# Fewer table passes on VectorE and ScalarE: sums by accumulating DMA, mixing on TensorE, contiguous kernel rows and a new instruction order in a gated mix of two long convolutions

## The chip, the cores and the metric

One core of a Trainium2 chip. The metric is device time in microseconds (us) of one execution; three runs of the kernel before took 291.55, 291.79 and 292.98, median 291.79. The engines are named as in the profile: PE is the matrix engine (PEld its weight loads), DVE the vector engine, ACT the scalar engine, POOL and SP the two others, which here build constants and issue DMAs.

## The reference

The input `x = A_u` (2048 steps, 448 channels) goes through two long convolutions, and a gate mixes them:

```python
x = A_u
g = sigmoid((x * gate_w).sum(-1, keepdims=True))
# A: kernel K[d, l] = Re sum_n C[d,n] * exp(dt*A[d,n] * l) * dt*B[d,n],  n = 0..255
a = causal_conv(x, K) + x * Dskip
# B: kv = (4-tap causal shift of k) * v
b = x * (causal_conv(kv, ssm_k) + kv * ssm_D)
out = g * a + (1 - g) * b          # bf16
```

The reference does the convolutions by real FFTs of length 4096.

## The kernel before, in words

Channels are cut into four quarters H = 0 to 3 of 112, that is NC = 28 columns on each of four groups; M = 8 x 28 = 224. The 2048 steps lie as 32 x 64. A convolution is a hand-made FFT by matmuls: `spread` (line 339) and `transform` (351) go forward, `swapped` (670) swaps real and imaginary halves by SP's DMAs, `products` (392) multiplies on DVE, `stage_a` (368) and `stage_b` (379) come back. Every result in PSUM (`ps`, four rooms of two banks) is taken out by an `evac`, a copy that class `Copies` (322) puts on ACT, or on DVE where the string `COPIES` has a V.

For convolution A the kernel rows must first be made, in one table per quarter (`table`, 842). `KGen.exps` (410) and `KGen.reals` (417) are exponentials on ACT of a (128, 224) row each: `reals` makes NR = 16 rows R[i] = exp(8(2i+1) x). `levels` (421) makes sines on ACT from phases on DVE. `tables` (471) builds two tables of 32 complex rows in bf16, TQ and TP, on DVE: `product` (439) multiplies n rows by one complex entry and leaves the four real products, `add` (446) sums them in pairs. Rows 8 to 15 of TP are such sums of four rows each, twice 128 x 1792 elements. `back` (464) makes rows 16 to 31 from rows 15 to 0, times R. `sums` (510) contracts TQ with TP on PE, `gather` (527) interpolates the result into kernel rows KT, laid out (b, r, n), and `cols` (566) gives `spread` row n of it, 64 elements that lie 28 apart, as weights. R and KT share the tile RK.

`mix` (876) does the mixing for a quarter: the window of `ug` (tile natv; it holds b) is multiplied by `og` = 1 - g, the window of `uu` (tile natu; it holds a) by `gb` = g, and they are added. For the last quarter `epilogue_A` (818) multiplies by g straight from PSUM, adds, and stores.

`Consts` (174) builds the transform matrices at the start: POOL writes integer ramps, DVE turns them into phases (`phases`, 203; used by `stage_2`, 224, and `stage_b`, 250, in passes of 128 x 1024), ACT takes sines. Where ACT goes from exponentials to sines or back, the trace has an ACT_TABLE_LOAD.

The order of the work is written out by hand. Every engine call is recorded (`Order`, 123), and the string `ORDER` gives the sequence in which they are issued; `issue` (130) chains the calls of one engine, SP's and POOL's among them, so each engine runs them in this order. `SLOTS` and `ROOMS` say which of six SBUF buffers (`q`) and four PSUM rooms each use gets. `PLAN` says in which order the parts are recorded: tables T, convolutions B and A, and mixing m. As all calls are issued at one place, the profile gives every instruction the same line, 135; the tile tells them apart.

Of the kernel before, what the change touches and what calls it, by code (L numbers as in the profile page):

```python
# [37 lines left out]
    "02143540432152033255104414002511354023"  # L38
)
ROOMS = (  # L40
    "102312011321221213030023033232221120301102302321010101233332311322223113013221223223032100113132320001003030031120131221"
    "11120010230212303030103220332020232303031012110011322201031010322120303131222023"
)
COPIES = (
    "SSVSSSSSSSSSSSSSSSSSSSSSSSSSSSSSSSSSSSSSSSSSSSSSSSSSSSSSSSSSSSSSSSSSSSSSSSSSSSSSSSSSSSSSSSSSSSSSSSSSSSSSSSSSSSSSSSSVVSSS"
    "SSSSSSSSSSSSSSSSSSSSSSSSSSSSSSSSSSSSSSSSSSSSSSSSSSSSSSSSSSSSSVSSSSVSSS"
)
ORDER = (
# [53 lines left out]
)  # L102

# [70 lines left out]
class Consts:  # L174
# [49 lines left out]
    def stage_2(self, b_col, off_col, room):  # L224
# [3 lines left out]
        for k0 in (0, 16):  # L228
            if k0:
                for r in range(2):  # L230
                    nc.vector.scalar_tensor_tensor(out=off_col[r], in0=b_col, scalar=32.0 * k0, in1=off_col[r], op0=ALU.mult, op1=ALU.add)
# [699 lines left out]
```

## Time and profile before

| what | value |
|---|---|
| median of three runs | 291.79 us |
| the profiled execution | 293.36 us, of it span 291.0 us |
| mean granted TensorE clock | 0.875 |
| DMA | 20.92 MB in 56755 packets, mean 72 GB/s |
| POOL | 53 instructions, 9.9 us, all in the first 37 us |
| DVE's longest waits | 7.0 us for PE, 5.5 for ACT (four), 4.7 for a DMA, all on tile q |
| stores | from about 277 us on; nothing but DMA after 280.4 us |

The page has the busy time and share of each engine; the span in 40 slices; the DMA queues; the chain that ended last, followed back from the end, with its share by engine; the costliest groups of instructions, as "line engine operation out<-in shapes xcount | busy us, mean ns of one | idle time before them and what ended it"; and DMA issues, with KB and us to landing. The trace behind it gives the same by stretch of time, by tile, or in order of time.

### The profile page before, as it was taken

The page shows a single profiled execution, that of the slowest core. Times are in us where ns is not written, and L with a number is a line of the kernel's source. Part 1 is how long each engine was busy: PE and PEld are TensorE (multiplying, and loading weights), DVE is VectorE, ACT ScalarE, POOL GpSimd, SP SyncE. Part 2 cuts the span into 40 slices and gives each one's busy share as a digit, 9 for nine tenths or more (in the row PEclk, how much of TensorE's full clock was granted, in tenths as well). Part 3 has the DMA queues.
Part 4 walks back from the last instruction along what each step waited for, and adds up shares of the span by engine and source line. Part 5 has one row for each costly group of instructions (what it writes and reads, how often), then busy time and mean ns, then how long its engine had stood idle before and what let it go on. Part 6 is the DMA issues. An engine that isn't in the chain of part 4 may idle for free.

```text
span 291.0 us, 12305 instructions
## 1 busy us (share of the span) xinstructions
PE 219.8 (76%) x5599; PEld 203.9 (70%) x5599; DVE 242.2 (83%) x374; ACT 224.3 (77%) x322; POOL 9.9 (3%) x53
## 2 busy tenths in 40 slices
PE   0155786878796998997699988687998967899820
PEld 0144775777786988996698978587998956789720
DVE  8869999999997699999789997893999985524950
ACT  3378949799887889999779899993999994268600
POOL 9100200000000000000000000000000000000000
PEclk9995879778796997999979999998999799669955
DMA  6999924915761002522300000622000036100067
GB/s 174 178 198 190 144 94 74 176 39 106 119 146 36 5 2 34 124 71 66 83 5 2 5 2 2 149 61 52 2 5 3 2 81 144 37 5 2 2 134 121
DMA packets 56755, 20.92 MB, mean 72 GB/s; under 512 B 49280, under 2 KB 56192, under 8 KB 56704
## 3 DMA queue, kind: packets, MB, share of 16 engines
q1 hardware_dynamic: 52192, 18.65, 34.5%
q10 hardware_dynamic: 4512, 1.49, 2.4%
q8 instruction: 44, 0.72, 1.0%
q14 instruction: 7, 0.06, 0.1%
HBM read 8.17 MB, written 2.52 MB: 37 GB/s over the span
## 4 chain that ended last, share of the span: by engine, by line
PE 35%; ACT 27%; DVE 22%; issue 7%; DMA 5%; POOL 0%; SPq 0%; ACTq 0%; DVEq 0%; POOLq 0%
PE ps L135 35%; ACT q L135 20%; DVE TP L135 6%; DVE TQ L135 4%; ACT RK L135 4%; DVE natv L135 3%; DMA q<-in_A_C_im_dram 2%; DVE q L135 2%; DMA q<-in_A_B_re_dram 2%; ACT ET L135 2%; DVE PH L135 1%; DVE ET L135 1%; DVE G L135 1%; ACT natu L135 1%; DVE RK L135 1%
## 5 line engine op out<-in xcount | busy, mean ns | idle before, releaser
L135 ACT CAST q<-ps 128x1024 bf16<-128x1024 f32 (+4 forms) x160 | 135.2, 937 | 8.5 <-PE ps L135 8.1
L135 PEld LDWEIGHTS <-q 128*128 128x128 bf16 (+2 forms) x720 | 56.0, 149 | 18.1 <-DMA q<-in_A_B_re_dram 13.5
L135 DVE TENSOR_TENSOR TQ<-TQ,ET 128x896 bf16<-128x896 bf16 (+1 forms) x56 | 44.6, 818 | 0.0
L135 PE MATMUL ps<-q,s_W 128*128 128x112 bf16 (+1 forms) x544 | 36.2, 221 | 10.9 <-ACT q L135 10.8
L135 PEld LDWEIGHTS <-s_W 128*128 128x128 bf16 x544 | 30.8, 103 | 15.3 <-issue 12.9
L135 PE MATMUL ps<-TP,TQ 128*32 128x32 bf16 x1792 | 32.8, 242 | 11.2 <-issue 9.9
L135 DVE TENSOR_TENSOR q<-q,q 128x3584 bf16<-128x3584 bf16 (+1 forms) x22 | 32.4, 1509 | 10.3 <-DMA q<-q 4.7
L135 PEld LDWEIGHTS <-TQ 128*32 128x32 bf16 x1792 | 30.7, 155 | 13.3 <-issue 12.3
L135 PEld LDWEIGHTS <-natu 128*32 128x32 bf16 (+1 forms) x560 | 30.4, 182 | 11.8 <-DMA natu<-in_B_k_dram 6.0
L135 PE MATMUL ps<-sa_R,q 128*128 128x128 bf16 x448 | 37.8, 250 | 1.0 <-ACT q L135 0.7
L135 DVE TENSOR_TENSOR TP<-TP,ET 128x3584 bf16<-128x3584 bf16 (+2 forms) x20 | 30.7, 1552 | 0.0
L135 PE MATMUL ps<-q,G 128*128 128x28 bf16 x1024 | 27.9, 176 | 2.3 <-ACT q L135 2.3
L135 PEld LDWEIGHTS <-G 128*128 128x128 bf16 x1024 | 27.2, 97 | 3.3 <-issue 2.6
L135 ACT ACTIVATE RK<-hold 128x224 bf16<-128x224 f32 x64 | 22.9, 410 | 3.5 <-DVE hold L135 1.4
L135 PE MATMUL ps<-q,natu 128*32 128x224 bf16 (+3 forms) x336 | 18.9, 332 | 8.7 <-DMA natu<-in_B_k_dram 5.4
L135 ACT CAST RK<-ps 128x896 bf16<-128x896 f32 (+1 forms) x15 | 10.9, 749 | 18.2 <-PE ps L135 18.2
L135 ACT ACT_TABLE_LOAD x16 | 20.5, 1283 | 2.0 <-PEq L915 1.7
L135 PE MATMUL ps<-Wc,natv 128*64 128x128 bf16 x224 | 16.1, 293 | 4.0 <-DVE natv L135 2.6
L135 PEld LDWEIGHTS <-natv 128*64 128x64 bf16 x224 | 15.6, 212 | 4.4 <-DVE natv L135 2.7
L135 PE MATMUL ps<-q,q 128*32 128x336 bf16 (+3 forms) x112 | 17.7, 329 | 1.2 <-DMA q<-in_B_k_dram 1.2
L135 ACT ACTIVATE ET<-PH 128x1344 bf16<-128x1344 int16 (+1 forms) x12 | 17.6, 1465 | 1.2 <-DVE PH L135 1.1
L135 DVE TENSOR_TENSOR TP<-TP 128x1792 bf16<-128x1792 bf16 (+4 forms) x22 | 18.0, 830 | 0.0
(76 smaller groups left out, 272.1 us busy)
## 6 DMA issues: line engine op xcount, KB each, us to landing
q<-q SPq DMA_DIRECT2D x64, 112.0 KB, 2.4
sk<-in_B_ssm_k_dram SPq DMA_DIRECT2D x16, 112.0 KB, 3.5
natv<-in_B_v_dram SPq DMA_DIRECT2D x4, 448.0 KB, 8.0
natu<-in_A_u_dram SPq DMA_DIRECT2D x4, 448.0 KB, 5.7
out_dram<-natv SPq DMA_DIRECT2D x8, 112.0 KB, 4.4
out_dram<-natv ACTq DMA_DIRECT2D x8, 112.0 KB, 4.8
xfd<-q SPq DMA_DIRECT2D x1, 672.0 KB, 3.3
hold<-xfd SPq DMA_DIRECT2D x2, 336.0 KB, 2.9
```

The source lines that it names most:

```text
L135: ins = f(*args, **kw)
```

## The change

Six edits, in one program.

1. Rows 8 to 11 and 12 to 15 of TP are no longer summed by DVE. `split` lets the product write one half of the real products into the rows themselves and the other half into rows 16 and up, and a DMA of POOL's queue adds the second to the first (`accum_op`). `back(8, 16)`, which needs rows 0 to 7, now stands ahead of `back(0, 8)`, which needs rows 8 to 15. There are two such DMAs in each of four tables.
2. `reals` takes 8 exponentials and one factor exp(128 x) on ACT, and DVE makes the other 8 rows by one product.
3. `og` is gone. A matrix `minus` = -identity is made once, and `stage_b` of convolution A begins each bank with a matmul of `minus` and the window of `ug`, so that PSUM holds a - b; `mix` multiplies by g and adds b. For the last quarter the passes with `og` go too.
4. KT is laid out (n, b, r), so that a kernel row is 64 elements in a row.
5. `Copies` becomes `Sides`: it also puts the phases of `stage_2` and `stage_b` on DVE or ACT. The string has 198 letters for what was 190 (eight phases more); four of the eight phases are on ACT, and six copies on DVE instead of five.
6. `SLOTS`, `ROOMS`, the string of sides and `ORDER` are all new, so that every engine's sequence changes, the loads on SP and the table loads on ACT (21 instead of 16) among them.

```diff
+    def line(self, dst, src, mult, add):
+        if self.vector():
+            self.nc.vector.tensor_scalar(out=dst, in0=src, scalar1=mult, scalar2=add, op0=ALU.mult, op1=ALU.add)
+        else:
+            self.nc.scalar.activation(dst, src, ACT.Identity, scale=mult, bias=add)
...
-def stage_b(nc, places, G, U, consume, banks=2):
+def stage_b(nc, places, G, U, consume, banks=2, less=None):
...
+            if less is not None:
+                for i in range(0, n, 16):
+                    nc.tensor.matmul(pt[:, h + i // 16, 0:448].rearrange("p (b c) -> p b c", c=NC), lhsT=less[0], rhs=less[1](b0 + 16 * h + i, 16),
+                                     start=True, stop=False)
...
     def reals(self, H):
-        for i in range(NR):
+        for i in range(NR // 2):
             self.nc.scalar.activation(self.R[:, i], self.hold[:, H % 2, 0], ACT.Exp, scale=float(8 * (2 * i + 1)))
+        self.nc.scalar.activation(self.R[:, NR], self.hold[:, H % 2, 0], ACT.Exp, scale=128.0)
+        self.nc.vector.tensor_tensor(out=self.R[:, 8:16], in0=self.R[:, 0:8], in1=self.R[:, NR].unsqueeze(1).to_broadcast([P, 8, M]), op=ALU.mult)
...
+    def split(self, dst, base, src, n, e):
+        T, r = self.TP, self.ET[:, ENTRY[e], 1]
+        o, s = T[:, dst], T[:, src]
+        part = list(o.ap[0])
+        self.nc.vector.tensor_tensor(
+            out=bass.AP(o.tensor, o.offset, [part, [2 * M, n], [M, 2], [(base - dst) * 2 * M, 2], [1, M]]),
+            in0=bass.AP(s.tensor, s.offset, [part, [2 * M, n], [0, 2], [M, 2], [1, M]]),
+            in1=bass.AP(r.tensor, r.offset, [list(r.ap[0]), [0, n], [-M, 2], [M, 2], [1, M]]), op=ALU.mult)
+        flat = lambda a: T[:, a:a + n].rearrange("p n c m -> p (n c m)")
+        self.nc.gpsimd.dma_start(out=flat(dst), in_=flat(base), accum_op=ALU.add)
...
-        p(16, 0, 4, 64)
+        self.split(8, 16, 0, 4, 64)
         add(TQ, 3, 15, 2, -2)
-        add(TP, 8, 16, 4)
         q(27, 1, 2, -1, 512)
-        p(24, 4, 4, 64)
+        self.split(12, 20, 4, 4, 64)
         add(TQ, 7, 27, 2, -2)
-        add(TP, 12, 24, 4)
         q(27, 5, 2, 2, 512)
+        self.back(8, 16)
+        add(TQ, 8, 27, 2)
         self.back(0, 8)
-        add(TQ, 8, 27, 2)
-        self.back(8, 16)
...
-                self.evac(KT[:, :, r + 1 - per:r + 1, w0:w1], room.rearrange("p r (b n) -> p b r n", b=8))
+                self.evac(KT[:, w0:w1, :, r + 1 - per:r + 1], room.rearrange("p r (b n) -> p n b r", b=8))
...
-        return self.KT[:, :, :, c].rearrange("p b r -> p (b r)")
+        return self.KT[:, c].rearrange("p b r -> p (b r)")
...
+    minus = wp.tile([P, P], bf16, name="minus")
+    V.tensor_scalar(out=minus[:], in0=ident, scalar1=-1.0, scalar2=None, op0=ALU.mult)
...
+    less = lambda H: (minus[:], lambda b0, n: window(ug, b0, n, H))
...
         if H == NQG - 1:
             V.tensor_tensor(out=o, in0=o, in1=x, op=ALU.mult)
-        weighed(o, og)
-        if H < NQG - 1:
-            weighed(x, gb)
-            V.tensor_tensor(out=o, in0=o, in1=x, op=ALU.add)
+            return
+        V.tensor_tensor(out=paired(x), in0=paired(x), in1=gb[:].unsqueeze(2).to_broadcast([P, 64, NC // 2, 2]), op=ALU.mult)
+        V.tensor_tensor(out=o, in0=o, in1=x, op=ALU.add)
```

More of the change, by code (lines that the diff above doesn't have):

```diff
@@ L37 @@
 SLOTS = (
-    "02143540432152033255104414002511354023"
+    "20134425014243155430102242331052105431"
 )
 ROOMS = (
-    "102312011321221213030023033232221120301102302321010101233332311322223113013221223223032100113132320001003030031120131221"
-    "11120010230212303030103220332020232303031012110011322201031010322120303131222023"
-)
-COPIES = (
-    "SSVSSSSSSSSSSSSSSSSSSSSSSSSSSSSSSSSSSSSSSSSSSSSSSSSSSSSSSSSSSSSSSSSSSSSSSSSSSSSSSSSSSSSSSSSSSSSSSSSSSSSSSSSSSSSSSSSVVSSS"
-    "SSSSSSSSSSSSSSSSSSSSSSSSSSSSSSSSSSSSSSSSSSSSSSSSSSSSSSSSSSSSSVSSSSVSSS"
+    "201203313031210032010020112210211213301123120030012333111101212122223332022113030333011103101230332230110323321100113330"
+    "00111301233103100130202120333303303332010030223122101210213321310131103103032103"
+)
+SIDES = (
+    "VSSSVVSVSSSSSSSSSSSSSSSSSSSSSSSSSSSSSSSSSSSSSSSSSSSSSSSSSSSSSSSSSSSSSSSSSSSSSSSSSSSSSSSSSSSSSSSSSVSSSSSSSSSSSSSSSSSSVSSS"
+    "VSSVSSSSSSSSSSSSSSSSSSSSSSSSSSSSSSSSSSSSSSSSSSSSSSSSSSSSSSSSSSSSSSSVSVSSSSSSSS"
 )
 ORDER = (
[53 rows of a table removed]
[51 rows of a table added]
 )
@@ L174, with __init__ @@
 class Consts:
-    def __init__(self, nc, pool, scratch):
-        self.nc, self.pool = nc, pool
+    def __init__(self, nc, pool, scratch, sides):
+        self.nc, self.pool, self.sides = nc, pool, sides
         self.scratch, self.used = scratch, 0
@@ L228, in stage_2 @@
         for k0 in (0, 16):
+            off = off_col
             if k0:
+                off = [self.carve(1).bitcast(f32) for _ in range(2)]
                 for r in range(2):
-                    nc.vector.scalar_tensor_tensor(out=off_col[r], in0=b_col, scalar=32.0 * k0, in1=off_col[r], op0=ALU.mult, op1=ALU.add)
+                    nc.vector.scalar_tensor_tensor(out=off[r], in0=b_col, scalar=32.0 * k0, in1=off_col[r], op0=ALU.mult, op1=ALU.add)
             ph = shaped(room, [16, 2, 64], i32, at=128 * k0)
             for r in range(2):
-                self.phases(ph[:, :, r, :], j.rearrange("p (k s) -> p k s", k=16), b_col, off_col[r])
+                self.sides.line(ph[:, :, r, :], j.rearrange("p (k s) -> p k s", k=16), b_col, off[r])
             nc.scalar.activation(W[:, k0:k0 + 16].rearrange("p k r s -> p k (r s)"),
@@ L258, in stage_b @@
                 nc.vector.tensor_scalar(out=o, in0=k_col, scalar1=256.0 * i, scalar2=turn, op0=ALU.mult, op1=ALU.add)
-                self.phases(ph[:, :, r, :], jv, k_col, o)
+                self.sides.line(ph[:, :, r, :], jv, k_col, o)
             tmp = shaped(room, [64, 32], at=to)
@@ L319, in col_of, with vector @@
         return self.sel[:, self.var[key]].rearrange("p a b -> p (a b)")
-class Copies:
+class Sides:
     def __init__(self, nc):
         self.nc, self.n = nc, 0
+    def vector(self):
+        self.n += 1
+        return SIDES[self.n - 1] == "V"
     def __call__(self, dst, src):
-        self.n += 1
-        if COPIES[self.n - 1] == "V":
+        if self.vector():
             self.nc.vector.tensor_copy(dst, src)
@@ L332, in __call__ @@
             self.nc.scalar.copy(dst, src)
+    def line(self, dst, src, mult, add):
+        if self.vector():
+            self.nc.vector.tensor_scalar(out=dst, in0=src, scalar1=mult, scalar2=add, op0=ALU.mult, op1=ALU.add)
+        else:
+            self.nc.scalar.activation(dst, src, ACT.Identity, scale=mult, bias=add)
 def rows_of(zs, k0, k1, c0, c1):
@@ L387, in stage_b @@
                 for r in range(2):
-                    nc.tensor.matmul(o, lhsT=G[:, b, r].rearrange("p g a -> p (g a)"), rhs=U[:, r, b], start=(r == 0), stop=(r == 1))
+                    nc.tensor.matmul(o, lhsT=G[:, b, r].rearrange("p g a -> p (g a)"), rhs=U[:, r, b], start=(r == 0 and less is None),
+                                     stop=(r == 1 and (less is None or i % 16 == 15)))
             consume(b0 + 16 * h, n, pt[:, h:h + banks, 0:448])
@@ L406, in __init__ @@
         self.ph = arena["PH"][:].bitcast(i32).rearrange("p (n t m) -> p n t m", t=2, m=M)
-        self.R = shaped(arena["RK"][:], [NR, M])
-        self.S, self.KT = shaped(arena["RK"][:], [32, NC]), shaped(arena["RK"][:], [8, 8, NC], at=32 * NC)
+        self.R = shaped(arena["RK"][:], [NR + 1, M])
+        self.S, self.KT = shaped(arena["RK"][:], [32, NC]), shaped(arena["RK"][:], [NC, 8, 8], at=32 * NC)
     def exps(self, H):
@@ L643, in body @@
     arena = {n: ar.tile([P, size], bf16, name=n) for n, size in (
-        ("natv", 7168), ("natu", 7168), ("sk", NC * 64), ("TQ", 64 * M), ("TP", 64 * M), ("ET", 30 * M), ("RK", NR * M), ("PH", 16 * M))}
+        ("natv", 7168), ("natu", 7168), ("sk", NC * 64), ("TQ", 64 * M), ("TP", 64 * M), ("ET", 30 * M), ("RK", (NR + 1) * M), ("PH", 16 * M))}
     G = ar.tile([P, 64, 2, 4, 32], bf16, name="G")
@@ L649, in body @@
     places = Places(ar, psum)
-    evac = Copies(nc)
+    evac = Sides(nc)
     def qt(shape, dtype=bf16):
@@ L678, in body @@
     nc.scalar.dma_start(ldt, A_log_dt.partition_broadcast(P))
-    cons = Consts(nc, wp, shaped(arena["TP"][:], [3584], i32))
+    cons = Consts(nc, wp, shaped(arena["TP"][:], [3584], i32), evac)
     cons.rows()
@@ L792, in body @@
     V.tensor_copy(gb[:], gt[:].unsqueeze(2).to_broadcast([P, 64, 2]))
-    og = wp.tile([P, 64, 2], bf16, name="og")
-    V.tensor_scalar(out=og[:], in0=gt[:].unsqueeze(2).to_broadcast([P, 64, 2]), scalar1=-1.0, scalar2=1.0, op0=ALU.mult, op1=ALU.add)
     def window(t, b0, n, H):
@@ L811, in body @@
     paired = lambda t: t.rearrange("p b (n t) -> p b n t", t=2)
-    weighed = lambda t, f, b0=0, n=64: V.tensor_tensor(out=paired(t), in0=paired(t), in1=f[:, b0:b0 + n].unsqueeze(2).to_broadcast([P, n, NC // 2, 2]), op=ALU.mult)
+    less = lambda H: (minus[:], lambda b0, n: window(ug, b0, n, H))
     def store(b0, n):
@@ L825, in epilogue_A, with conv @@
         return consume
-    def conv(terms, consume):
+    def conv(terms, consume, less=None):
         U = qt([2, 64, NC])
         stage_a(nc, places, R, U, terms, evac, eights)
-        stage_b(nc, places, G, U, consume)
+        stage_b(nc, places, G, U, consume, less=less)
     def conv_B(H):
@@ L865, in conv_A @@
             transform(nc, places, W2, K, evac)
-            conv(products(nc, X, S, K), held(uu, H))
+            conv(products(nc, X, S, K), held(uu, H), less(H))
             return
@@ L873, in conv_A @@
             stage_a(nc, places, R, U, (X, S), evac, [range(c0, c0 + 8), range(c0 + 8, c0 + CB)])
-        stage_b(nc, places, G, U, epilogue_A(H), 1)
+        stage_b(nc, places, G, U, epilogue_A(H), 1, less(H))
     def mix(H):
```

104 rows, old and new, of the table ORDER are left out of this document.

## The prediction

> **What bounds the kernel now.** First the busy shares and the shares of the chain that ended last, from the page:
>
> ```profile
> PE 219.8 (76%) x5599; PEld 203.9 (70%) x5599; DVE 242.2 (83%) x374; ACT 224.3 (77%) x322; POOL 9.9 (3%) x53
> PE 35%; ACT 27%; DVE 22%; issue 7%; DMA 5%; POOL 0%; SPq 0%; ACTq 0%; DVEq 0%; POOLq 0%
> ```
>
> No engine is the bound alone, so I cut the span at four points read from the order of time (the upper P pass of the first table ends at 83 us, that of the fourth at 238, the last DVE instruction at 280) and asked for busy time by stage:
>
> ```profile
> 0.00:83.00 83.00, 51.22 (x1010) 46.26 (x1010) 78.29 (x161) 61.73 (x88) 9.92 (x53) 0.84 0.80 136
> 83.00:240.00 157.00, 135.52 (x3542) 126.47 (x3537) 140.09 (x184) 141.81 (x208) 0.00 (x0) 0.93 0.18 41
> 240.00:280.00 40.00, 33.10 (x1058) 31.21 (x1056) 23.44 (x31) 20.79 (x28) 0.00 (x0) 0.83 0.18 41
> ```
>
> After the stretch come PE, PEld, DVE, ACT, POOL, then granted clock, DMA share, GB/s. Up to 83 us DVE is the bound (78.3 of 83). In the middle three engines are at 86 to 90%, and the chain there alternates: PE 44%, ACT 43%, of it 7% (11.0 us) on tile RK: by the order of time some 2 us of copies of kernel rows and 9 us, or 30 of 48, of the real exponentials of tables 1 to 3. From 240 to 280 PE bounds; from 280 the last stores go out, untouched by the change.
>
> Prices come from groups kept apart by shape, except where the chain gives a pace, that is start to start, which is shorter because neighbours overlap:
>
> ```profile
> L135 DVE TENSOR_TENSOR TP<-TP 128x1792 bf16<-128x1792 bf16 x12 | 12.8, 1085 | 0.0
> L135 DVE TENSOR_TENSOR natv<-natv,og 128x1792 bf16<-128x1792 bf16 x4 | 4.3, 1083 | 0.0
> L135 DVE TENSOR_SCALAR TQ<-TP 128x1024 int32<-128x1024 int32 x8 | 7.3, 931 | 0.0
> L135 ACT ACTIVATE RK<-hold 128x224 bf16<-128x224 f32 x64 | 22.9, 410 | 3.5 <-DVE hold L135 1.4 <-PE ps L135 1.2 <-DVE TP L135 0.9
> L135 ACT ACT_TABLE_LOAD x16 | 20.5, 1283 | 2.0 <-PEq L915 1.7
> ```
>
> ```profile
> 60.92 1.00 DVE TP L135
> 68.60 3.88 DVE TP L135 x2
> 165.26 1.79 ACT RK L135 x6
> ```
>
> So on the path a DVE pass of 1792 bf16 elements costs 1.00 us, one of 3584 1.94, a real exponential 0.30.
>
> **Part by part.** *Upper P rows.* Per table two adds of 1792 leave DVE: 8 x 1.00 = 8.0. The two products stay at 1.94: `split` only writes the halves elsewhere, in runs of 224, and the pairs of TQ written in such runs cost the same as flat ones (0.54 per 896). Eight DMAs of 448 KB from POOL's queue come in. Each waits for its product; nothing else stands on POOL by then. The new wait is that of `back(0, 8)` on both. Queued behind it on DVE are the next conv's products and phases, and PE's sums of that table wait for it. The order listing shows what covers the second DMA, between its product and that pass: in table 0 12 instructions, 7.8 us by pace, then 9.1, 16.6 and 8.0. How long such a DMA takes no row shows. The nearest:
>
> ```profile
> hold<-xfd SPq DMA_DIRECT2D x2, 336.0 KB, 2.9
> natv<-in_B_v_dram SPq DMA_DIRECT2D x4, 448.0 KB, 8.0
> ```
>
> Low end 2.9, a plain copy on quiet queues; high end 16, twice the 8.0 of loads in full queues, as an addition reads its target too. The middle stage moves 18% DMA, so I take the quiet row twice, 6 us: hidden, with 2 us to spare.
>
> *Exponentials.* ACT loses 7 per table: 28 x 0.30 = 8.4. DVE gains one product of 1792 per table, 4.0. Its wait is for ACT's last exponential, and `back(8, 16)` is behind it; the listing puts 2 to 4 us between.
>
> *Mixing.* DVE loses `og` (0.1) and four passes, 4.0, and makes `minus` once (0.1, the row of `og`). PE gains 16 matmuls of 448 columns. The nearest row has 112 columns on a full tile:
>
> ```profile
> 71.02 1.47 PE L135 MATMUL ps<-q,s_W 128*128 128x112 bf16 x24 [0.84 <-ACT q L135]
> 214.15 1.20 PE L135 MATMUL ps<-WcK,RK 128*64 128x128 bf16 x16
> 45.80 0.64 PE L135 MATMUL ps<-Wc,sk 128*64 128x128 bf16 x16
> ```
>
> 24 in 1.47 with 0.2 of latency is 55 ns each, so four times as many columns make 0.22, and 16 make 3.5 (by the 128x448 row on 32-wide tiles, 0.47: 7.5; below by nothing, as they are all new work). They wait for conv B's window, ready long before in tables 0 to 2.
>
> *Contiguous rows.* The other two lines are one spread with strided weights and one with contiguous ones: (1.20 - 0.29)/15 = 61 ns against (0.64 - 0.22)/15 = 28. The page's PEclk is 9 in both slices. So 33 ns x 224 = 7.4 us of PE go. The copies now write (n, b, r): 0.80 per 896, and the copies that scatter 1024 into q pay the same per element (0.90), so nothing.
>
> *Setup passes, copies.* Four passes of 1024 go from DVE to ACT, 4 x 0.72 by pace = 2.9 less on DVE while ACT is 44% busy. One more copy and larger ones on DVE: +1.6.
>
> *Order.* ACT's listing has 21 table loads where there were 16: one in setup, four in the middle, 4.9 us at 1.22 pace. They stand between the RK copies of the tables, where ACT waits anyway (us in total, times, longest):
>
> ```profile
> ACT RK L135 <- PE ps L135: 24.6, 10, 6.3
> ```
>
> I put 1.2 of the 4.9 on the path. The Trainium skill ("ScalarE: Activation LUTs", Table sets) says to batch activations by set and gives about 2.7 us a load; by that figure five loads would be 13.5 us and the gain below would vanish if all were on the path, but the rows here say 1.28. On SP, the B and C loads move ahead of A's, whose last is now behind the first two transposes; A's products come at DVE's 15th us of work, so this is free, and DVE loses the 3.4 us wait for the mask row and gains about 2 for the B and C transposes. The v loads (SP) stay last before the first spread.
>
> **The sum**, by stage. Setup: DVE's listing summed by pace up to `back(0, 8)` of table 0 falls from 76.6 to 72.9 us, and the wait by 1.4; but the first sums on PE come at 83.4 behind an ACT copy as well, so I take -3.5 (0 to -5). Middle: DVE is level (136.6 and 136.5), so ACT and PE decide: of the 21 exponentials that go, 30/48 or 13 lie on the chain, -3.9; loads +1.2; PE (three spreads -5.5, twelve `minus` +2.6) x its share 0.44 = -1.3: -4.0 (ends +6, the new order losing more than that, and -9, all of it counting). Tail: 56 matmuls of the last spread -1.8, four `minus` +0.9, half on the path: -0.5; the `og` pass there hid behind PE. Together -8.0 on the profiled execution's 293.4 (span 291.0 and 2.4 around it): 285.4. That execution is 1.6 above the median 291.79, so 283.8, rounded to **284**.
>
> **The rivals.** *The accumulating DMA lands late (slower).* Covers of 7.8, 9.1, 16.6 and 8.0 mean that each us beyond 8 costs up to three: the 8 gained are gone at about 11. At 12 the waits are 4.2 + 2.9 + 0 + 4.0 = 11.1: **295**. For it: the row at 8.0 for the same size. Against: that row is of a stage with 80% DMA. Chance 0.13; at 16 us the waits are 23 and the time 307.
>
> *The order gives it back.* With three engines near 90%, 1.5 us per table of new waiting between PE, ACT and DVE and all five loads on the path (+5) leave **291**. For it: every buffer is reassigned. Chance 0.14.
>
> *Everything counts.* Setup -5, middle -9, tail -2: **276**. Chance 0.13.
>
> *POOL and DVE collide.* DVE's first 1024-pass took 1.80 while POOL was filling tiles, the next ones 0.80:
>
> ```profile
> 2.85 1.80 DVE L135 TENSOR_SCALAR TQ<-TP 128x1024 int32<-128x1024 int32 x1
> 4.83 0.80 DVE L135 TENSOR_SCALAR TQ<-TP 128x1024 int32<-128x1024 int32 x1
> ```
>
> If POOL's issuing holds DVE as long, 8 x 1.0 = 8: **291.5**. Chance 0.05. The Trainium skill ("SBUF — State Buffer", Summary and Who interferes with whom) speaks against this change: descriptor generation on GpSimd is starved while VectorE is in its fast modes, and a DMA to hide under VectorE work should come from another queue; it excepts tensor_tensor, which is most of what runs there. The 1.80 agrees with it as far as POOL's fills go; no run here shows a DMA of POOL's.
>
> *It does not do what it says* (products in four-part patterns at half rate, 8 x 1.9 = 15: **298**). Against: the TQ pairs above. Chance 0.03.
>
> **How the numbers follow.** Forecast 0.52 (279 to 289), everything counts 0.13, order 0.14, DMA late 0.13, collision 0.05, not as said 0.03. Range 275 to 296: below it some 0.05, above it 0.11 from the late DMA and the half rate. A difference under 0.5% (290.3 to 293.2) is what a measurement here cannot tell from none. Faster: 0.52 + 0.13 + 0.07 of the order case = 0.72; same 0.07 of the order case and 0.02 of the collision, 0.09; slower 0.19, the rest.
>
> **What would show it.** DMA issues of POOL landing under 8 us and no wait of DVE's TP<-TP,RK on a DMA; first sums on PE near 79 us instead of 83.4; matmuls on RK near 220 ns instead of 290; 21 table loads, the later ones ahead of RK copies that wait less; split products at 2.0 us. I am wrong if DVE waits for DMAs on TP, if the split products are slower, or if PE and ACT idle more in the middle stage than the 21 and 15 us they do now.

## The result, and the profile after

The changed kernel takes **270.44 us** (median of four runs, 269.28 to 272.71) against 292.38 for the kernel before on the same chip (291.55 to 295.35): a ratio of 0.924 (95% interval 0.915 to 0.933). I forecast 284.0 and a range of 275 to 296; the direction was right, the gain nearly three times as large as forecast and outside the range. Times here and below are medians of all runs of a kernel; ratios and intervals leave out the few runs over 1.5% above the fastest of their kernel, and are to the runs of before beside it on the same chip.

The profiled execution took 269.95 us (span 268.2). The page's busy line and its shares of the chain:

```profile
PE 206.4 (77%) x5615; PEld 189.3 (71%) x5615; DVE 232.4 (87%) x363; ACT 225.8 (84%) x302; POOL 14.7 (5%) x61
PE 37%; DVE 20%; ACT 19%; SPq 12%; issue 6%; DMA 1%; ACTq 0%; DVEq 0%
```

PE lost 13.4 us of work and DVE 9.8, and ACT gained 1.5, but the span lost 22.8. So each of the three also lost idle time, PE 9.4 us, DVE 13.0 and ACT 24.3. (SPq's 12% is setup, almost all of it: the chain now begins with SP issuing loads up to 33 us.) The stages are cut here at the first sums on PE of table 0 and of table 3, near the 83 and 240 us of the prediction. Columns: stretch, length, then PE, PEld, DVE, ACT, POOL, granted clock, DMA share, GB/s. First the kernel after:

```profile
0.00:79.00 79.00, 47.99 (x975) 43.09 (x979) 74.93 (x158) 67.15 (x86) 9.55 (x55) 0.86 0.83 153
79.00:220.50 141.50, 126.44 (x3563) 117.06 (x3564) 136.84 (x180) 135.76 (x187) 5.14 (x6) 0.97 0.30 64
220.50:258.00 37.50, 31.98 (x1090) 29.12 (x1090) 20.64 (x27) 22.86 (x31) 0.00 (x0) 1.00 0.24 54
```

then the middle of the kernel before, cut at the same events:

```profile
83.40:240.70 157.30, 135.72 (x3540) 126.72 (x3541) 140.39 (x184) 142.13 (x208) 0.00 (x0) 0.93 0.18 41
```

In the middle DVE was idle for 157.3 - 140.4 = 16.9 us before and is for 4.7 after; ACT for 15.2 and 5.7. ACT's longest waits in these two stretches, before and after (us in total, times, longest):

```profile
ACT RK L135 <- PE ps L135: 9.9, 5, 4.8
ACT q L135 <- PE ps L135: 4.0, 9, 0.9
...
ACT RK L133 <- PE ps L133: 3.9, 4, 1.5
ACT q L133 <- PE ps L133: 0.7, 4, 0.3
```

The 24.6 us that the prediction quotes for ACT's wait for kernel rows are those of the whole span; 9.9 of them lie in the middle, and 3.9 are left there. What the edits themselves did shows in the groups by shape (the first row is before's, the others after's), and below them in the page's DMA issues:

```profile
L135 PE MATMUL ps<-WcK,RK 128*64 128x128 bf16 x224 | 16.4, 296 | 1.4 <-DVE natv L135 0.6 <-ACT RK L135 0.4 <-issue 0.3
...
L133 ACT ACT_TABLE_LOAD x21 | 26.9, 1283 | 2.6 <-DVE TP L133 2.1
...
L133 DVE TENSOR_TENSOR TP<-TP,ET 128x3584 bf16<-128x3584 bf16 x12 | 24.1, 2019 | 0.0
...
L133 PE MATMUL ps<-WcK,RK 128*64 128x128 bf16 x224 | 9.0, 221 | 2.2 <-ACT q L133 1.9 <-ACT RK L133 0.3
...
L133 PE MATMUL ps<-natv,minus 128*128 128x448 bf16 x16 | 4.7, 353 | 0.9 <-ACT q L133 0.9
```

```profile
TP<-TP POOLq DMA_DIRECT2D x8, 448.0 KB, 4.5
```

The matmuls on kernel rows went from 296 to 221 ns, the split products kept their 2.02 us, and a DMA lands 4.5 us after its issue. By stage, from the start to the first sums, to the sums of table 3, to the start of the last `stage_b` matmul, and to the end of the span:

| | setup | middle | tail | rest |
|---|---|---|---|---|
| before | 83.4 | 157.3 | 37.1 | 13.2 |
| after | 78.9 | 141.5 | 36.0 | 11.8 |
| difference | -4.5 | **-15.8** | -1.1 | -1.4 |
| forecast | -3.5 | **-4.0** | -0.5, both | |

In the two other profiles of after (after_again and after_5 below) the middle takes 143.3 and 142.2 us, so the -15.8 is good to some 2 us.

### The profile page after: what moved, and what is told of

Read it like the earlier page. It is cut to its first block, busy times and chain, and to the rows that moved or that the text cites. A ratio compares the mean times of both kernels' runs of the same rounds, so it can differ in the third digit from the quotient of the medians.

```text
span 268.2 us, 12358 instructions
## 1 busy us (share of the span) xinstructions
PE 206.4 (77%) x5615; PEld 189.3 (71%) x5615; DVE 232.4 (87%) x363; ACT 225.8 (84%) x302; POOL 14.7 (5%) x61
## 4 chain that ended last, share of the span: by engine, by line
PE 37%; DVE 20%; ACT 19%; SPq 12%; issue 6%; DMA 1%; ACTq 0%; DVEq 0%
PE ps L133 37%; ACT q L133 14%; SPq L133 12%; DVE TQ L133 6%; DVE TP L133 5%; DVE q L133 3%; DVE natv L133 2%; ACT ET L133 2%; ACT RK L133 2%; ACT L133 1%; DVE ET L133 1%; DVE RK L133 1%; DMA sk<-in_B_ssm_k_dram 1%; DVE PH L133 1%; DMA q<-q 0%
## 5 line engine op out<-in xcount | busy, mean ns | idle before, releaser
L133 ACT CAST q<-ps 128x1024 bf16<-128x1024 f32 (+3 forms) x158 | 133.1, 922 | 15.1 <-PE ps L133 13.5
L133 PEld LDWEIGHTS <-q 128*128 128x128 bf16 (+2 forms) x720 | 51.6, 144 | 17.9 <-DMA q<-in_A_B_re_dram 8.2
L133 PEld LDWEIGHTS <-natu 128*32 128x32 bf16 (+1 forms) x560 | 29.6, 179 | 13.0 <-issue 6.3
L133 PE MATMUL ps<-q,s_W 128*128 128x112 bf16 (+1 forms) x544 | 33.6, 213 | 5.2 <-ACT q L133 4.8
L133 PE MATMUL ps<-sa_R,q 128*128 128x128 bf16 x448 | 33.6, 232 | 1.4 <-ACT RK L133 0.8
L133 PEld LDWEIGHTS <-s_W 128*128 128x128 bf16 x544 | 27.8, 99 | 8.8 <-issue 7.3
L133 PE MATMUL ps<-q,natu 128*32 128x336 bf16 (+3 forms) x336 | 18.8, 332 | 10.6 <-DVE natv L133 5.8
L133 ACT CAST RK<-ps 128x448 bf16<-128x448 f32 (+1 forms) x16 | 11.5, 725 | 7.0 <-PE ps L133 7.0
L133 POOL DMA_DIRECT2D TP<-TP x8 | 7.0, 877 | 179.1 <-DVE TP L133 55.7
L133 DVE TENSOR_TENSOR TP<-TP,RK 128x3584 bf16<-128x3584 bf16 x8 | 16.0, 2014 | 0.0
```

Of the source, the lines that this page charges most:

```text
L133: ins = f(*args, **kw)
```

## The experiments

The question is why the middle gave 15.8. **Theory 1**: the new order fills idle time by itself, and the edits add their prices. **Theory 2**: with three busy engines every removed us counts, whatever the order. **Theory 3**: an order suits the durations it was made for, so that the halves are worth little apart. **Theory 4**, which came later, is that after's order is so tight that any removed work counts. In the edits below `joined(n)` puts the last n recorded calls at one place of the order and `skip()` records nothing at a place, so that the numbers in ORDER stay valid.

| kernel | time, us | ratio to before (95%) | middle | idle there: DVE, ACT |
|---|---|---|---|---|
| before | 292.4 | 1 | 157.3 | 16.9, 15.2 |
| after | 270.4 | 0.924 (0.915 to 0.933) | 141.5 | 4.7, 5.7 |
| after_again | 271.3 | 0.928 (0.921 to 0.935) | 143.3 | 6.5, 7.3 |
| after_5 | 271.1 | 0.925 (0.920 to 0.929) | 142.2 | 5.2, 6.7 |
| order_alone | 284.4 | 0.968 (0.964 to 0.973) | 150.2 | 7.4, 8.4 |
| order_alone2 | 284.7 | 0.973 (0.968 to 0.978) | 151.2 | 10.3, 8.9 |
| edits_alone | 290.9 | 0.988 (0.984 to 0.993) | 156.7 | 19.0, 19.9 |
| edits_alone2 | 293.0 | 0.997 (0.994 to 1.001) | 160.6 | 23.4, 21.4 |
| no_dma | 275.7 | 0.937 (0.932 to 0.943) | 145.8 | 3.5, 8.1 |
| no_exp | 278.0 | 0.946 (0.942 to 0.950) | 148.2 | 12.1, 6.7 |
| no_exp2 | 277.8 | 0.950 (0.944 to 0.956) | 147.5 | 11.9, 6.2 |
| no_rows | 276.2 | 0.940 (0.933 to 0.946) | 145.9 | 9.0, 9.3 |
| no_phases | 272.1 | 0.925 (0.918 to 0.932) | 142.0 | 5.4, 6.2 |
| no_minus | 269.3 | 0.920 (0.914 to 0.926) | 143.2 | 6.5, 7.3 |
| no_minus5 | 269.7 | 0.917 (0.913 to 0.920) | 142.5 | 5.5, 6.6 |
| b_dma | 296.5 | 1.012 (1.008 to 1.017) | 159.2 | 24.7, 17.2 |
| b_exp | 292.7 | 0.997 (0.993 to 1.001) | 157.0 | 13.9, 18.7 |
| less_act | 270.2 | 0.923 (0.916 to 0.931) | 142.2 | 5.0, 11.5 |
| less_dve | 271.0 | 0.926 (0.920 to 0.933) | 143.0 | 10.3, 7.4 |
| more_act | 299.3 | 1.022 (1.015 to 1.029) | 162.9 | 22.5, 13.5 |

Where I give us "over after" below, it is the ratio less 0.926, the mean of after's three series, times 293; the intervals make that good to some 2 us.

### Which half: the order or the operations

*order_alone*: after's strings, before's operations. The edits are those of no_dma, no_exp, no_rows, no_phases and no_minus below, in one kernel.

> After's order, buffers and copy sides (its strings ORDER, SLOTS, ROOMS and the copy part of SIDES) with before's operations: the upper P rows are added on VectorE at the place of each DMA, all 16 real exponentials on ScalarE beside those that stay, the weighing passes on VectorE just ahead of the other mixing pass, kernel rows strided, all eight phase passes on VectorE. Of the 22.0 us between 292.4 and 270.4, theory 1 (the order packs the engines, the edits add their direct prices only) expects about 15: 277 (274 to 281). Theory 2 (with three engines near 90% every removed us counts, the order only arranges them) expects 288 to 294. Theory 3 (an order is made for the durations it was planned with, so either half alone is worth little) expects 286 or more here and in the next run.

Measured 284.4. In this kernel, in edits_alone and in no_exp some instructions overwrote values that others had still to read, which changes part of the computation and adds waits of its own. So all three were made again.

*order_alone2*:

```diff
-        self.S, self.KT = shaped(arena["RK"][:], [32, NC]), shaped(arena["RK"][:], [NC, 8, 8], at=32 * NC)
+        self.S, self.KT = shaped(arena["RK"][:], [32, NC]), shaped(arena["RK"][:], [8, 8, NC], at=64 * NC)
...
+        at = [(i,) for i in range(8)] + [(), tuple(range(8, 16))]
+        for own in at:
+            for j in own:
+                self.nc.scalar.activation(self.R[:, j], self.hold[:, H % 2, 0], ACT.Exp, scale=float(8 * (2 * j + 1)))
+            self.nc.joined(len(own))
```

> The run order_alone once more with its dependencies cleaned: there, exponentials of the next table overwrote kernel rows that the spread had still to read, so PE had waits that neither kernel has. Now the strided rows lie in the place of the late exponentials, those eight go to ScalarE where after's product stood, and back(0, 8) comes first as in before. All of before's operations, after's order. It stood at 284.4 against 294.0. If the false waits had cost much it is now under 281 and theory 1 is nearer; the first reading (order worth 9 to 10 us, not 15) expects 282 to 287.

Measured 284.7, ratio 0.973. The false waits had cost little. The new order is worth 2.7%, 8 us, with the old operations: not theory 1's 15, and not theory 2's nothing. Its middle, and ACT's waits for kernel rows there:

```profile
82.50:233.70 151.20, 133.09 (x3547) 125.01 (x3547) 140.91 (x185) 142.35 (x209) 0.00 (x0) 0.93 0.18 41
```

```profile
ACT RK L141 <- PE ps L141: 3.5, 3, 1.5
```

DVE and ACT do the work of before (140.4 and 142.1 us there) in 6.1 us less. The wait for rows is 3.5 us against 9.9 before and 3.9 after: it went with the order, not with the operations.

*edits_alone* and *edits_alone2*: before's strings, after's operations.

```diff
-        p(16, 0, 4, 64)
+        self.split(8, 16, 0, 4, 64)
...
-        add(TP, 8, 16, 4)
+        self.gain(8, 16, 4)      # the accumulating DMA, at the addition's place
...
+        self.nc.vector.tensor_tensor(out=self.R[:, 8:16], in0=self.R[:, 0:8], in1=self.R[:, NR].unsqueeze(1).to_broadcast([P, 8, M]), op=ALU.mult)
         self.back(8, 16)
+        self.nc.joined(2)
```

> Before's order, buffers and copies with after's operations: the DMAs stand where the adds stood, eight exponentials and a product of 1792 ahead of back(8, 16), minus matmuls at the head of each bank, contiguous rows, four phase passes on ScalarE. Theory 1 expects 284 to 287 (my sum without the order). Theory 2 expects 276 (273 to 280). Theory 3 expects 286 or more. Covers of the accumulating DMAs are those of before's list between add and back, which are shorter: a wait of back(0, 8) on them would show as DVE TP <- DMA TP.

Measured 290.9. Its four phase passes were on ACT already: its trace has `TQ<-TP 128x1024 int32` four times on ACT, so the next expectation is wrong to call them missing. What edits_alone2 changes is the place of the mask product in table 0, and in table 3 that of the new product and `back(8, 16)`, which go right behind `back(0, 8)`.

> The run edits_alone once more, now with the four phase passes on ScalarE as well (they were missing), and with table 0's mask product for WcK ahead of the second split product, which overwrote its operands. All of after's operations, before's order. It stood at 290.9 against 294.0. Theory 2 expected 276 and is already in trouble; theory 3 (either half alone is worth little) expects 287 to 291; my sum without the order expected 284 to 287.

Measured 293.0, ratio 0.997: nothing. Theory 2 falls, and with it my sum without the order (284 to 287). Theory 3 is nearest, though by the medians it misses too: it named 286 or more for the order (284.7) and 287 to 291 here.

Its middle, the same waits there, and one of DVE's:

```profile
84.80:245.40 160.60, 130.62 (x3547) 120.81 (x3547) 137.24 (x180) 139.18 (x190) 5.13 (x6) 0.92 0.27 59
```

```profile
ACT RK L143 <- PE ps L143: 11.3, 3, 4.4
DVE TP L143 <- DMA TP<-TP: 3.7, 1, 3.7
```

Against before's middle, PE has 5.1 us less work, DVE 3.2 and ACT 3.0, and the stage is 3.3 us longer: DVE idles 23.4 us instead of 16.9, ACT 21.4 instead of 15.2. The freed time became waiting; 3.7 us of DVE's is one wait of `back(0, 8)` for an accumulating DMA, which the section on one edit alone takes up. Alone the order gives 8 us and the operations 1; together they give 22. No kernel has the other operations without those DMAs in before's order, so the 1 us may hide a gain of the others behind the DMAs' loss. b_dma alone is 1.2%, 3.6 us, slower; with that given back it would be 289, still above my 284 to 287.

### What each edit is worth in after's order

*no_dma*:

```diff
-        self.nc.gpsimd.dma_start(out=flat(dst), in_=flat(base), accum_op=ALU.add)
+        self.nc.vector.tensor_tensor(out=flat(dst), in0=flat(dst), in1=flat(base), op=ALU.add)
```

> After with one thing undone: the eight accumulating DMAs are additions of 1792 on VectorE at the same places (8 x 1.00 = 8.0 us of VectorE). Theory 1 expects +2 to +4 (272 to 274), since VectorE idles some 5 us in the middle and waits elsewhere. Theory 2 expects all 8.0: 278 (277 to 280).

3.4 us over after: the 8.0 us of DVE count by less than half.

*no_exp* and *no_exp2*: all 16 exponentials on ACT, no product.

> After with one thing undone: all 16 real exponentials a table on ScalarE (8 more and one factor fewer, 28 x 0.30 = 8.4 us more on ScalarE), and no product of 1792 on VectorE (4 x 1.0 less). Theory 1 expects +1 to +3 (271.5 to 273.5), theory 2 +4 to +6 (274 to 277), as ScalarE's 8.4 count and VectorE's 4.0 come back.

> The run no_exp once more with its dependencies cleaned: four of the eight exponentials follow those of rows 4 to 7, the other four go where the product stood. All 16 real exponentials on ScalarE, else after. It stood 6.5 us over after. Theory 1 expects +1 to +3; theory 2 +4 to +6 (274 to 277); more than 8.4 would say that the order breaks, not only that the work counts.

*no_exp* measured 278.0. *no_exp2* is 7.2 over after, more than either theory had: ACT's 8.4 us count almost in full, and the 4.0 that DVE is spared bring nothing back that shows.

*no_rows*: KT strided, in the place of the late exponentials (the first edit of order_alone2, with the copies and `cols` of before).

> After with the kernel rows strided again (in the place of the late exponentials, which in after's order are free then). PE's matmuls on RK go back from 28 to 61 ns start to start, 224 x 33 ns = 7.4 us. The runs so far leave 3.6 us of order_alone2's 14.1 over after for this edit and the phases together (14.1 less 3.8 for the additions, 7.6 for the exponentials, -1.1 for the mixing), if the edits add up: theory 3 as it now stands expects +1.5 to +3 (272 to 273.5). If PE's us counted in full it would be 277.

4.1 over after, more than expected. The matmuls on kernel rows are at 290 ns again (296 in before, 221 in after):

```profile
L141 PE MATMUL ps<-WcK,RK 128*64 128x128 bf16 x224 | 16.3, 290 | 1.8 <-ACT q L141 1.1 <-ACT RK L141 0.7
```

So 7.3 us of PE's time in that group are worth 4.1 us. Its tail and rest take 49.9 us (50.3 in before; 47.8, 47.4 and 47.6 in after's three profiles), so about 2 of the 4.1 lie behind the middle.

*no_phases*: the first eight letters of the string of sides are V.

> After with all eight phase passes of the setup on VectorE (four more passes of 1024, 4 x 0.72 by pace = 2.9 us, where VectorE bounds up to 79 us). By the setup's own bound +2 to +3 (272.5 to 273.5); if the setup has slack that the first table's waits take up, 0 to +1. Whatever it is, it should show in the start of the first sums (78.9 in after) and not behind.

The first sums start at 80.8 instead of 78.9, as expected, but the ratio is after's (0.918 to 0.932, some 2 us each way). The stage shows the edit, the time does not.

*no_minus*, and the same kernel again as no_minus5, in one series with after_5:

```diff
-                    nc.tensor.matmul(pt[:, h + i // 16, 0:448].rearrange("p (b c) -> p b c", c=NC), lhsT=less[0], rhs=less[1](b0 + 16 * h + i, 16),
-                                     start=True, stop=False)
+                    nc.skip()
...
+        weighed(o, og)
+        weighed(x, gb)
+        nc.joined(2)
```

> After with the mixing undone: no minus matmuls (16 x 0.35 = 5.6 us less on PE by the trace of after), four weighing passes on VectorE (4 x 1.08) beside the passes that stay. By the direct prices PE's loss and VectorE's gain nearly cancel: theory 1 expects -1 to +2 (269.5 to 272.5), theory 2, by which each engine's us counts in part, -1 to +3.

> After as it is, as the base on this chip, so that the two kernels with less work are set against runs of the same call: 269 to 272, a ratio of 0.915 to 0.933 to before.

> The kernel no_minus again (after with the weighing passes on VectorE in place of the 16 minus matmuls), five rounds. If the mixing edit gains nothing, as all four of its passes lay in the tail behind PE, while its 16 matmuls add 5.6 us to PE's work: 1 to 2 us under after_5, 268.5 to 270. If the first reading was chance: within 0.7 us of it.

> After as it is, five rounds, as the base of no_minus5 on the same chip: 269.5 to 272, a ratio to before of 0.92 to 0.93, as in the two earlier series (0.9242 and 0.928).

0.917 (0.913 to 0.920) against 0.925 (0.920 to 0.929) on the same chip: the edit costs, by the medians 1.4 us, by the ratios 2.4. In before the four passes with `og` stood at 240.2, 242.2, 272.7 and 273.7 us, in the tail, where DVE works 23 of 40 us. Taking them out gained nothing that shows, and 16 matmuls came to PE, eight of them in the tail that PE bounds. Twelve of the 16 run in pairs:

```profile
150.94 0.55 PE L133 MATMUL ps<-natv,minus 128*128 128x448 bf16 x2
251.42 0.35 PE L133 MATMUL ps<-natv,minus 128*128 128x448 bf16 x1
```

So one follows the other after 0.20 us, and the group takes 4.7 us, not the 5.6 of the expectations, which is 16 times the length of a single one. The kernel without this edit, at 269.3 and 269.7, is the fastest here by the median.

Undone one by one, the edits are worth 3.4 + 7.2 + 4.1 - 0.2 - 2 = 12.5 us; all undone at once (order_alone2), 13.8. In after's order they nearly add up.

### One edit alone in before's order

*b_dma* is the first two pairs of lines of the diff of edits_alone2, *b_exp* its last lines, with the eight exponentials and the factor in `reals`.

> Before with one thing done: the eight additions on upper P rows are accumulating DMAs, at the additions' places in before's order (in table 0 the mask product for WcK goes ahead of the second split product). 8.0 us leave VectorE. If a removed us of VectorE counts as in after's order (+3.8 when put back), -4: 288.5. Theory 3 expects 0 within 2 us (291 to 294.5), the freed time turning into idle time of VectorE in the middle (16.9 in before, over 20 here), because the instructions behind wait for PE and ScalarE, whose order is unchanged.

> Before with one thing done: eight of 16 real exponentials a table are one factor and a product on VectorE, just ahead of back(8, 16). 8.4 us leave ScalarE, 4.0 come to VectorE. As in after's order (7.6 when undone) it would be -7: 285.5. By my forecast's price of the chain (-3.9 for ScalarE) 288 to 290. Theory 3 expects 291 to 296: VectorE's product stands where the order has no room for it.

*b_dma* is 1.2% slower. Its middle, the wait that it made and its DMAs:

```profile
86.10:245.30 159.20, 133.74 (x3539) 124.45 (x3540) 134.53 (x178) 142.02 (x208) 5.12 (x6) 0.96 0.27 58
```

```profile
DVE TP L143 <- DMA TP<-TP: 5.0, 1, 5.0
```

```profile
TP<-TP POOLq DMA_DIRECT2D x8, 448.0 KB, 5.5
```

It is also above theory 3's 291 to 294.5. In the middle DVE has 5.9 us less work and 7.8 us more idle time. 5.0 of that is one wait of `back(0, 8)` for a DMA in table 1. In this order the two DMAs of a table are issued 1.7 to 2.5 us apart, not 4 to 9 as in after, and land in 4.3 to 7.9 us instead of 4.2 to 5.4. So my rival of the late DMA is real, in the order that leaves it no cover.

The DMAs of table 0 also delay a load. Between 70 and 84 us, before and in b_dma:

```profile
natu<-in_A_u_dram SPq DMA_DIRECT2D x1, 448.0 KB, 5.3
...
natu<-in_A_u_dram SPq DMA_DIRECT2D x1, 448.0 KB, 7.6
```

This load of `x` is issued at 72.1 us, between the two accumulating DMAs (71.7 and 74.2), and lands at 79.6 instead of 77.0 in before; PE's first matmul on it starts at 79.9 instead of 77.2, and the first sums at 86.1 instead of 83.4. So the setup, too, is 2.7 us longer. In edits_alone2 the same load takes 8.0 us, in b_exp and more_act, which have before's order without these DMAs, 5.1 and 5.0. In after the loads of `x` nearest to them are issued at 51.8 and 54.0 us, and the DMAs of table 0 at 65.2 and 69.3.

*b_exp* gained nothing. Its middle, and ACT's waits for kernel rows there:

```profile
83.90:240.90 157.00, 133.34 (x3540) 124.27 (x3540) 143.13 (x187) 138.30 (x190) 0.00 (x0) 0.94 0.18 43
ACT RK L143 <- PE ps L143: 11.9, 5, 5.1
```

ACT has 3.8 us less work and idles 3.5 us more, 2.0 of it in these waits (9.9 us before). DVE has 2.7 us more work. This is how I read it: the exponentials that I counted on the path stand ahead of copies that wait for PE anyway.

### Was the order fitted to its durations?

*less_act*, *less_dve* (after) and *more_act* (before):

```diff
 # less_act
+            if i > 3 or (H and i):
+                self.nc.skip()
 # less_dve
-        self.back(8, 16)
+        self.nc.skip()
 # more_act
+            n = 2 if i >= 9 else 1
+            for _ in range(n):
                 self.nc.scalar.activation(self.R[:, i], self.hold[:, H % 2, 0], ACT.Exp, scale=float(8 * (2 * i + 1)))
```

> After with more work taken from ScalarE: 25 of its 32 real exponentials below the factor are left out (rows 4 to 7 in table 0, rows 1 to 7 in tables 1 to 3; their rows keep what lay there), 25 x 0.30 = 7.5 us. If the order was fitted to its durations (theory 3 as first put), no gain beyond 1.5 us: 269 to 271. If the order is packed and ScalarE is on the path nearly all the time (theory 4), -3 to -6: 264.5 to 267.5, the mirror of +7.6 for putting 8.4 back.

> After with more work taken from VectorE: the pass back(8, 16) of each table is left out (4 x 1.94 = 7.8 us by pace; the upper rows keep what lay there). Theory 3 as first put: 268.5 to 271. Theory 4: -4 to -8 (262.5 to 266.5), as VectorE idles only 4.7 us of the middle.

> Before with 28 real exponentials done twice (rows 9 to 15 of each table), 8.4 us more on ScalarE, nothing else changed. Taking such work out of before gained nothing (0.997). The time of a fixed order can only grow more steeply the longer an instruction gets, so at least 0; theory 4 (before's path runs through waits between engines that the durations hardly set) expects +1 to +4 (294 to 297); a path on which the exponentials lie as in my chain reading (30 of 48) expects +4 to +5.

On one chip *less_act* has a ratio of 0.923, *less_dve* of 0.926 and after_again of 0.928. That is 1.4 and 0.5 us of gain (1.1 and 0.3 by the medians), within the intervals and short of theory 4's 3 to 6 and 4 to 8. Theory 4 falls. The middles of less_act and less_dve:

```profile
79.10:221.30 142.20, 126.89 (x3555) 117.71 (x3555) 137.16 (x180) 130.69 (x166) 5.13 (x6) 0.98 0.30 63
```

```profile
78.40:221.40 143.00, 127.31 (x3555) 117.94 (x3555) 132.72 (x178) 135.61 (x187) 5.13 (x6) 0.99 0.30 63
```

ACT has 5.1 us less to do than in after and idles 5.8 more; DVE 4.1 less (two of the four passes lie in the middle), and idles 5.6 more. *more_act*, before with 8.4 us more on ACT, takes 2.2% or 6.4 us longer (4.3 to 8.5 by the interval), where the theories reached from 0 to +5. So for work on ACT both orders behave alike: added work costs most of its length (before 6.4 of 8.4 us, after 7.2 of 8.4), removed work returns next to nothing (before 0.8 +- 1.2 of 8.4, with 4.0 put on DVE in exchange, after 1.4 of 7.5). Work added to the two others in after's order costs about half: DVE's 3.4 of 8.0, PE's 4.1 of 7.3. And one removal did pay: no_minus takes 4.7 us off PE, puts four passes on DVE and gains 1.4 to 2.4. That is theory 3 in the main, with one addition: after's order is also 8 us better on before's own durations.

## Why the prediction was wrong

**The step that failed is the middle, -4.0, which measured -15.8.** Three of its terms were wrong. That the kernel did become faster is no merit of the sum: without the new order its operations gave 0.8 us (edits_alone2), and the order stood in the sum as a cost.

*The order.* I treated it as a risk only (ends +6 to nothing) and priced its table loads, +1.2. It was a gain: 6.1 us of the middle with before's operations. I had quoted ACT's 24.6 us of waits for kernel rows, but read the figure of the whole span as that of the middle, where it is 9.9, and used it only as cover for the loads. It was also room that a new order could fill, as were DVE's 16.9 idle us: with before's operations the new order took the 9.9 to 3.5. The floor of the stage is the work of its busiest engine, 142 us before and 137 after; after's 141.5 lies near it, and my -4.0 left the stage at 153. Of the five more table loads, which I put at one in setup and four in the middle, three are in setup and two in the middle (8 before, 10 after). Their own cost was not taken apart: order_alone2 has 20 of them and is faster all the same.

*The exponentials, -3.9.* I multiplied removed time by its share of the chain. In before's order they are worth nothing (b_exp), in after's 7.2 us (no_exp2). The chain shows one path. In b_exp the time taken off ACT came back as its waits, which I read as a second path of nearly the same length, one that stays until the sequences of the engines are set anew.

*DVE level, 0.* The sum has DVE's work in the middle unchanged (136.6 and 136.5), new products against additions that leave, us for us. The trace has 140.4 us before and 136.8 after: six additions of 1792 are gone (-6.5) and three products have come (+3.3). Nor are their us worth the same: in after's order the additions are worth 3.4 of their 8.0 us (no_dma), and no_exp2, without the products, shows nothing for their 4.0.

**What held, and what was mis-sized.** Setup gave -4.5 for -3.5, and DVE's wait for the mask row is gone as said. PE's terms held: the contiguous rows stood at -5.5 x 0.44 and half of -1.8, together -3.3, and measured -4.1; the `minus` matmuls at +2.6 x 0.44 and half of 0.9, together +1.6, and measured +1.4 to +2.4. The accumulating DMAs took 4.5 us for my 6 (bounds 2.9 to 16) and no DVE instruction waited for one. The Trainium skill ("SBUF — State Buffer", Who interferes with whom) warns that descriptor generation on GpSimd is starved under VectorE's fast modes; here POOL's issues took 0.88 us each and the landings stayed within 4.2 to 5.4 us, but every DVE pass beside those issues is a tensor_tensor, which the page excepts, so the trace does not speak against it. The split products cost 2.02 us as before (2.02); the matmuls on contiguous rows went from 16.4 to 9.0 us, the 7.4 forecast. A `minus` matmul follows another after 0.20 us for my 0.22, and the 16 take 4.7 us for 3.5, as four stand alone at 0.35. The four passes that left DVE, 4.0 us in my list, brought nothing that shows. The 21 table loads came as listed, at 1.283 us each, and from the end of the instruction before one to the start of the next it is 1.30 to 1.31 us, with one exception of 1.52. The Trainium skill's 2.7 us ("ScalarE: Activation LUTs", Table sets) is not what they take here. The tail and the stores gave -2.5 for -0.5; by no_rows some 2 us of that go with the contiguous rows, of which the sum took half of 1.8.

**The rivals.** The DMA late: not in after, but so in b_dma. POOL and DVE collide: no; the DVE passes beside the eight issues are within 2% of their usual times, and in before the passes at 0.80 us that the prediction sets against the one at 1.80 also ran beside fills of POOL's, smaller ones. Half rate: no, as the split products show. The order gives it back: the opposite. Everything counts (276): nearest in time, wrong in its reason, as edits_alone2 shows. My last line named PE and ACT idling more in the middle than 21 and 15 us as a sign of being wrong; they idled 15 and 6, and nothing in the sum priced that side. Two of the rivals' own sums do not come out: the terms of the order (1.5 a table, 5 for loads of which 1.2 were counted) give 292 to 294 and not 291, and 284 and 15 at half rate give 299 and not 298.

**The clock** does not explain it. The granted clock of the middle rose from 0.93 to 0.97, but after's four runs, at 0.920, 0.923, 0.932 and 0.958, have spans of 270.9, 268.2, 269.2 and 267.5, and the best run of no_minus (266.2) had 0.913. A run of before at 0.937 still has a span of 287.8. order_alone2 won its 6.1 us in the middle at 0.93.

**What stays open**: which part of the order (queues, buffers, rooms or the place of the loads) gives the 8 us, and what the operations would give in before's order without the accumulating DMAs. The sequences of the engines depend on each other, and no kernel with one of them alone was tried.

## What to carry to other kernels

Where several engines are busy for 85 to 90% of a stage and the order is written out, the idle time of the busiest engine is a gain that a new order can reach: put the floor (the largest busy time of the stage) at the low end of the range, beside the sum of removed durations. Here removed work in an order that stayed was mostly worth little, and work added in that stage between 0.4 and 0.85 of its length, so the chain's share priced neither; an edit that takes work off one engine should be judged with the order made for it. Look also at when the removed instruction ran: the passes with `og`, in a stage bounded by PE, gave nothing back that shows. And a DMA that replaces engine work needs cover for its own landing, and can delay the loads issued beside it.

## What the runs showed of the hardware that I had not expected

An accumulating DMA from SBUF to SBUF of 448 KB lands 4.5 us after its issue when alone (4.2 to 5.4), less than the 8.0 of a load of that size in the busy setup, and up to 7.9 when a second one starts 2 us behind it. In b_dma a load of 448 KB issued between two of them landed after 7.6 us instead of 5.3. A pass that turns 1024 int32 ramps into phases takes ACT 1.24 us and DVE 0.81, so four of them moved 3.2 us off DVE for 4.8 on ACT.
